# Head 0 in an order written out by hand, in a kernel for clustered attention and routed experts

## The chip, the cores and the metric

One core of one Trainium2 chip runs the whole kernel. The metric is the device time of one execution in microseconds (us), median of the runs of one kernel. The trace of one profiled execution stands beside it. Engines are named PE (TensorE), DVE (VectorE), ACT (ScalarE), POOL (GpSimd) and SP (SyncE, which issues most DMAs).

## What is computed

Attention in which a query sees only the keys of its own cluster, and behind it a mixture of eight experts with one expert for each token. Cut to what matters:

```python
# q, k, v: (2, 8, 768, 64); centroids: (8, 16, 64)
q_assign = argmax(normed(q) @ normed(centroids))   # likewise k_assign
mask = q_assign[..., :, None] == k_assign[..., None, :]
scores = where(mask, scale * q @ k.T, -1e9)
scores = scores - max(scores, -1)
attn = exp(scores); attn /= sum(attn, -1) + 1e-9
x = (attn @ v)                                     # to (1536 tokens, 512)
expert = argmax(x @ w_gate); gate = softmax(x @ w_gate)[expert]
out = gate * (relu(x @ w1[expert]) @ w2[expert])   # first 384 tokens of an expert, else 0
```

## The kernel before

The 16 (batch, head) items are called heads 0 to 15, and two of them, which lie in the two halves of the 128 partitions, a pair. A head has 768 queries and 768 keys: six tiles of 128 and two halves of 384.

For every head the kernel holds four arrays. `W` (high part of q, rows that hold the cluster mark) and `Y1` (high part of k, marks scaled by a large number) give masked scores by one matmul; `Qs` and `Y0` carry the low parts, and one row of `Qs` holds minus the maximum of each query, so that a second matmul into the same bank subtracts it. In the order listings these names carry buffer numbers: W_94, Y_98, Qs_102 and Y_106 belong to head 0, W_96, Y_100, Qs_104 and Y_108 to head 1, W_95, Y_99, Qs_103 and Y_107 to head 2, and W_97, Y_101, Qs_105 and Y_109 to head 3.

The work of one head:

- **Splitting** (`split`, steps 0 to 3): ACT copies the high parts (64x768), POOL subtracts the low parts in three pieces of 64x256 (`ql`, `Y0`), and SP issues DMAs that put pieces where the matmuls need them.
- **Clusters**, for a pair: scores against the centroids, arg-maxima on DVE (`cl_assign`: `cmx`, `ceq`, a product, `cm`, one-hot rows `ohb`), turned by six transposes on PE (`ctb`), scaled by one ACT instruction (`qkm`), and sent by four DMAs into the mark rows of `W` and `Y1` (`cl_back`).
- **Maxima** (`max_tile`): 12 times a matmul `m` (128x384) and a maximum over it on DVE (`mx`). Heads 1 to 15 join the 12 columns in `mxx`, turn them on PE (`mtp`), copy them with ACT (`mr`) and send the row to `Qs` by a DMA that SP issues (`max_chain`, `max_rows`). Head 0 does it in halves, without a DMA: `mxp` on DVE, transposes `mtd`, an ACT copy into `Qs`.
- **Scores** (`st_group`, 12 groups): two matmuls `s` into one bank, and ACT's exponential into `pf`.
- **Values** (`pv_batch`, two batches of six matmuls `o`) and **sums of rows** (`p_add` on DVE gives `acc`; `sum_strips`, eight matmuls `rsp`), then scaling and the way to the experts.

The main loop runs over heads i and groups g. In a group it issues the scores of head i, one maximum of a later head (two where (i, g) is in `TWICE`; the list `maxima` runs on over the heads), and what `hooks(i, g)` hangs there: the second batch of values of head i - 1, its additions and its sums at g = 2 (`G_B1`), the first batch of head i at g = 8 (`G_B0`; for head 0 at g = 11).

Order: the prologue is written in program order (`manual_schedule`). In head 0 a scheduler sets the order of all engines. From head 1 on `keep` holds PE, DVE and ACT to program order (`held`); POOL and SP stay with the scheduler. PSUM has three banks for `s` (`psS`), two for `m` (`psM`), one for `o` and `mtd` (`psO`) and two for the rest (`psT`), so a third `m` waits for the maximum of the first. `keep_warm` issues matmuls on ones (128x128) whose results nobody reads.

After head 15 come the experts, whose weights are loaded four blocks ahead; their loads are issued at fixed places of the program.

## Time and profile before

| | us |
|---|---|
| median of 3 runs | 473.61 (469.14 to 473.76) |
| profiled execution | 472.46 |
| its span, first to last instruction | 470.3 |

The profile's page counts PE busy for 444.9 us (95% of the span), DVE for 321.4, ACT for 272.7 and POOL for 138.5. A busy PE means that matmuls are under way, not that they run at the peak rate. In the timeline rows below the first number is the start in us from the start of the span, the second the time until the last of the row ends, and x the count of instructions; a matmul of full float32 is counted as two. The bracket at a row's end is the idle time of the engine ahead of it, and what ended that.

### The profile page before, as it was taken

To read this page: it belongs to the slowest core of one execution; us is meant where nothing else is said; L and a number is where in the kernel's file an instruction comes from. 1 tells how busy PE (TensorE), PEld (TensorE's weight loads), DVE (VectorE), ACT (ScalarE), POOL (GpSimd) and SP (SyncE) were. 2 spreads that over 40 slices of the span, in tenths; PEclk is the share of its full clock that TensorE was granted. 3 is DMA by queue.
4 is the path that set the end of the run, shared out by engine and by line. 5 is a ranking of instruction groups with operands and counts; after the bars stand their busy time and mean duration, and the time that the engine had idled before them with its cause. 6 is when DMAs were issued, how large, how long until landed. Compare 5 with 4: busy or idle time off the path is not lost. (4 is left out here: it accounts for less than half of the span.)

```text
span 470.3 us, 8149 instructions
## 1 busy us (share of the span) xinstructions
PE 444.9 (95%) x2832; PEld 346.0 (74%) x2832; DVE 321.4 (68%) x682; ACT 272.7 (58%) x548; POOL 138.5 (29%) x168
## 2 busy tenths in 40 slices
PE   8899999999999989999999978999999999999984
PEld 7764766576666656667755556899999999899963
DVE  6785868678686795787754565587867777687411
ACT  4752655565666555566564624577786868586430
POOL 6793345736334356433000130001010101011010
PEclk9998999999999999999999999999999999999998
DMA  8366449976341514423112058659697878865110
GB/s 281 87 172 214 148 94 344 340 220 231 85 118 35 161 50 147 130 45 88 42 50 91 17 203 307 206 175 289 234 276 252 252 259 238 260 212 204 37 36 18
DMA packets 31223, 78.14 MB, mean 166 GB/s; under 512 B 4678, under 2 KB 5024, under 8 KB 31172
## 3 DMA queue, kind: packets, MB, share of 16 engines
q1 hardware_dynamic: 26340, 61.33, 43.4%
q0 software_dynamic: 4832, 16.15, 8.9%
q8 instruction: 30, 0.49, 0.4%
q14 instruction: 21, 0.17, 0.1%
HBM read 50.46 MB, written 16.76 MB: 143 GB/s over the span
## 5 line engine op out<-in xcount | busy, mean ns | idle before, releaser
L342 DVE TENSOR_REDUCE mx<-m 128x1 f32<-128x384 f32 x192 | 102.5, 553 | 54.1 <-PE m L335 52.2
L400 ACT ACTIVATE pf<-s 128x384 f32<-128x384 f32 x192 | 90.6, 492 | 54.8 <-PE s L396 49.9
L137 DVE TENSOR_TENSOR ws<-wraw,ws 128x1024 fp32r<-128x1024 f32 x64 | 78.1, 1223 | 32.2 <-ACT ws L131 32.0
L395 PE MATMUL s<-W,Y 112*128 112x384 f32 (+1 forms) x192 | 73.7, 384 | 2.0 <-ACT pf L400 2.0
L335 PE MATMUL m<-Y,W 112*128 112x384 f32 (+1 forms) x192 | 68.6, 361 | 5.0 <-DVE mx L342 3.1
L909 PE MATMUL g<-xc,ws 128*128 128x416 f32 x224 | 70.0, 373 | 1.2 <-PEq L1046 0.3
L131 ACT ACTIVATE ws<-wraw 128x1024 fp32r<-128x1024 f32 x64 | 67.0, 1050 | 4.5 <-DMA wraw<-in_w_dram 4.5
L909 PE MATMUL g<-hc,ws 128*128 128x416 f32 x224 | 69.5, 371 | 0.0
L649 POOL DMA_INDIRECT out_dram<-y,row x17 | 18.0, 1057 | 171.5 <-ACT pt L917 110.9
L415 PE MATMUL o<-pf,v 128*64 128x384 f32 x360 | 66.2, 496 | 0.4 <-DVE r L457 0.4
L396 PE MATMUL s<-Qs,Y 97*128 97x384 f32 (+1 forms) x192 | 65.7, 342 | 0.4 <-issue 0.3
L910 PE MATMUL g<-xc,ws 128*128 128x208 f32 x224 | 58.1, 259 | 1.0 <-issue 1.0
L910 PE MATMUL g<-hc,ws 128*128 128x208 f32 x224 | 57.9, 259 | 0.0
L298 POOL TENSOR_TENSOR ql<-qv,W 64x256 fp32r<-64x256 f32 x45 | 39.9, 912 | 51.3 <-ACT W L311 26.2
L298 POOL TENSOR_TENSOR Y<-kv,Y 64x256 fp32r<-64x256 f32 x48 | 41.4, 889 | 43.3 <-ACT Y L316 42.0
L395 PEld LDWEIGHTS s<-W,Y 112*128 112x128 f32 (+1 forms) x192 | 36.5, 190 | 23.2 <-issue 16.6
L917 ACT ACTIVATE pt<-g 128x208 f32<-128x208 f32 x84 | 27.5, 340 | 32.0 <-PE g L910 27.9
L335 PEld LDWEIGHTS m<-Y,W 112*128 112x128 f32 (+1 forms) x192 | 36.5, 191 | 12.9 <-DVE mx L342 8.1
L909 PEld LDWEIGHTS g<-xc,ws 128*128 128x128 f32 x224 | 42.1, 188 | 3.3 <-issue 2.9
L415 PEld LDWEIGHTS o<-pf,v 128*64 128x64 f32 x360 | 23.4, 137 | 28.3 <-issue 24.8
L910 PEld LDWEIGHTS g<-xc,ws 128*128 128x128 f32 x224 | 42.8, 191 | 1.2 <-issue 1.2
L910 PEld LDWEIGHTS g<-hc,ws 128*128 128x128 f32 x224 | 42.7, 191 | 0.0
(206 smaller groups left out, 700.6 us busy)
## 6 DMA issues: line engine op xcount, KB each, us to landing
wraw<-in_w_dram SPq DMA_DIRECT2D x64, 512.0 KB
xd<-z POOLq DMA_DIRECT2D x7, 780.0 KB
row<-xd SPq DMA_DIRECT2D x18, 260.0 KB
qv<-in_qT_dram SPq DMA_DIRECT2D x8, 384.0 KB
kv<-in_kT_dram SPq DMA_DIRECT2D x8, 384.0 KB
v<-in_v_dram SPq DMA_DIRECT2D x8, 384.0 KB
Y<-Y SPq DMA_DIRECT2D x32, 96.0 KB
Qs<-W SPq DMA_DIRECT2D x16, 192.0 KB
```

The lines of the kernel that those rows point to most:

```text
L131: keep(nc.scalar.activation(out=w[:, 0], in_=raw[c], func=AF.Copy))
L137: keep(nc.vector.tensor_tensor(out=w[:, 1], in0=t, in1=w[:, 0].bitcast(F32), op=ALU.subtract))
L298: keep(eng.tensor_tensor(out=out[:, cc], in0=a[:, cc], in1=b[:, cc].bitcast(F32), op=ALU.subtract))
L335: keep(nc.tensor.matmul(out=m[:, 0:HALF], lhsT=W[0:KA[h % 2], t * P:(t + 1) * P], rhs=Y1[0:KA[h % 2], j * HALF:(j + 1) * HALF], start=True ...
L342: keep(nc.vector.tensor_reduce(out=mxt[h][:, j, t:t + 1], in_=m[:, 0:HALF], axis=AX.X, op=ALU.max))
L395: keep(nc.tensor.matmul(out=s[:, 0:HALF], lhsT=Y1[0:ka, ks], rhs=W[0:ka, qs], start=True, stop=False))
L396: keep(nc.tensor.matmul(out=s[:, 0:HALF], lhsT=Y0[0:kb, ks], rhs=Qs[0:kb, qs], start=False, stop=True))
L400: keep(nc.scalar.activation(out=pt[h, u][:, slot[0], slot[1]], in_=s[:, 0:HALF], func=AF.Exp, scale=1.0 / float(D) ** 0.5))
L415: keep(nc.tensor.matmul(out=ot[h][j * D:(j + 1) * D, 0:HALF], lhsT=vt[h // 2][:, h % 2, kt, :], rhs=pf[:, n, j], start=(kt == 0), stop=(kt ...
L909: nc.tensor.matmul(out=o, lhsT=w[0], rhs=x.rearrange("p o n -> p (o n)"), start=start, stop=False)
L910: nc.tensor.matmul(out=o[:, 0:RW], lhsT=w[1], rhs=x[:, 0], start=False, stop=stop)
L917: nc.scalar.activation(out=t, in_=o[:, RW:2 * RW], func=AF.Copy)
```

## The change

Head 0 leaves the main loop, and a function `opening` issues it in an order written by hand; `held` is set from its start, so PE, DVE and ACT follow program order there too.

- In the prologue the clusters of the second pair are assigned at once, on DVE, ahead of head 0's maxima (before: in four steps spread over head 0). The first copy of head 1's `W` moves ahead of the marks of head 0's keys, and these are written by one ACT instruction instead of one on DVE and one on ACT. The small constants `trib`, `ebr`, `dlr` and `run0` move from DVE to POOL, into the prologue.
- Head 0's 12 maxima and head 1's 12 come first on DVE. The two additions of head 0 and the maxima of head 2 stand behind them. Head 0's first batch of values starts behind the scores, the second stands in `opening` too instead of in head 1, with three maxima of head 2 between its pieces; two more stand between the sums in head 1. One maximum moves from the opening to group 8 of head 2.
- The split of head 2 begins in the prologue; that of head 3 follows behind head 0's scores, with its step 0 ahead of the row of head 1's maxima (`max_rows(1)`).
- 13 of the `keep_warm` matmuls go: 2 of 6 around head 0's key transposes, 1 of 4 among the first six maxima, 4 of 6 ahead of the first `mtd`, and the 6 among head 1's maxima.

```diff
     WARM1 = 1
-    WARM2 = 6
+    WARM2 = 2
     G_B0, G_B1, G_TURN, G_OUT = 8, 2, 5, 11
-    TWICE = {(0, g) for g in range(6)} | {(1, 2), (2, 2), (3, 2)}
+    TWICE = {(1, 2), (2, 2), (2, 8), (3, 2)}
...
-    def cl_back(pi):
-        tb = psT.tile([P, S], BF16, tag="t", name="ctb")
+    tb_t = {}
+
+    def cl_back_turn(pi):
+        tb = tb_t[pi] = psT.tile([P, S], BF16, tag="t", name="ctb")
         for t in range(NT):
             keep(nc.tensor.transpose(tb[:, t * P:(t + 1) * P], ohb[:, t, :], idb))
+
...
         if step == 0:
-            keep(nc.scalar.activation(out=W[a], in_=d["q"][a], func=AF.Copy))
+            if high:
+                keep(nc.scalar.activation(out=W[a], in_=d["q"][a], func=AF.Copy))
             ql[h] = work.tile([P, S], R32, tag="ql", name="ql", bufs=2)
             minus(eng, ql[h][a], d["q"][a], W[a])
...
-    def max_part(h, j, pool=psO, tag="o"):
-
-        mx = work.tile([P, TH], F32, tag="mxp", name="mxp")
+    def max_half(h, j):
+        mx = mxt[h, j] = work.tile([P, TH], F32, tag="mxp", name="mxp")
         ts = slice(j * TH, (j + 1) * TH)
         keep(nc.vector.tensor_tensor(out=mx, in0=mxt[h][:, 0, ts], in1=mxt[h][:, 1, ts], op=ALU.max))
+        if j == 1:
+            mxt.pop(h)
+
+    def half_row(h, j, warm=0):
+        mx = mxt.pop((h, j))
         br = MROW[h % 2]
-        tp = pool.tile([P, 512], F32, tag=tag, name="mtd")
-        if j == 0 and h == 0:
-            keep_warm(WARM2, tp)
+        tp = psO.tile([P, 512], F32, tag="o", name="mtd")
+        if warm:
+            keep_warm(warm, tp)
         for t in range(TH):
             keep(nc.tensor.transpose(tp[0:1, t * P:(t + 1) * P], mx[:, t:t + 1], ident))
         keep(nc.scalar.activation(
             out=pick(Qs_t, h)[br:br + 1, j * HALF:(j + 1) * HALF], in_=tp[0:1, 0:HALF], func=AF.Copy, scale=-1.0
         ))
-        if j == 1:
-            mxt.pop(h)
...
-    def pv_batch(h, u):
-        if u == 0:
+    def pv_batch(h, u, ns=range(TH)):
+        if (u, ns[0]) == (0, 0):
         pf = pt[h, u]
-        for n in range(TH):
+        for n in ns:
...
-    def sum_strips(h):
...
+            if between:
+                between()
...
         ebr, dlr = (const.tile([P, E], BF16, name=n) for n in ("ebr", "dlr"))
-        keep(nc.vector.memset(ebr, 0.0))
-        keep(nc.vector.memset(dlr, 0.0))
-        keep(nc.vector.tensor_copy(ebr[0:1], cs[0:1, C_EB:C_EB + E]))
+        nc.gpsimd.memset(ebr, 0.0)
+        nc.gpsimd.memset(dlr, 0.0)
+        nc.gpsimd.tensor_copy(ebr[0:1], cs[0:1, C_EB:C_EB + E])
...
-        if i == 0:
-            if g < 4:
-                next(gens["c"], None)
-            if g == 4:
-                cl_back(1)
-            if g in (2, 3, 4, 5):
-                split(2, g - 2)
-            if 6 <= g < 10:
-                split(3, g - 6)
...
         if g == G_B1 and i > 0:
-            pv_batch(i - 1, 1)
+            if i > 1:
+                pv_batch(i - 1, 1)
             if i > 1 and i != H + 2:
                 out_scale(i - 2)
-            p_add(i - 1, 1)
-            sum_strips(i - 1)
+            if i > 1:
+                p_add(i - 1, 1)
+            sum_strips(i - 1, ahead if i == 1 else None)
...
+        nc.gpsimd.tensor_copy(trib, cs[:, C_TRI:C_TRI + P])
+        first_rows()
...
-        cl_scores(1, 3, NT // 2, NT // 2 + 1)
+        cl_scores(1, 3, NT // 2, NT)
         split(0, 2)
+        cl_back0("k", tk)
         keep_warm(4, psM.tile([P, 512], F32, tag="m", name="warm"))
-        cl_back0("k", tk)
-        keep_warm(2, psM.tile([P, 512], F32, tag="m", name="warm"))
-        mask0("k", tk, 0, slice(0, HALF), nc.vector)
-        mask0("k", tk, 0, slice(HALF, S), nc.scalar)
+        nc.scalar.activation(out=pick(W_t, 1)[MAIN[1]], in_=pair[0]["q"][MAIN[1]], func=AF.Copy)
+        mask0("k", tk, 0, slice(0, S), nc.scalar)
+        for _ in cl_assign(1, nc.vector):
+            pass
         split(0, 3)
+        split(1, 0, high=False)
+        split(1, 1)
         mask0("q", tq, 1, slice(0, S), nc.scalar)
         mask0("k", tk, 1, slice(0, S), nc.scalar)
-        split(1, 0)
-        split(1, 1)
...
+        for k in range(NT):
+            first_max(k)
+        max_half(0, 0)
+        split(2, 0)
         for j in range(2):
             one_row(j, 1)
-        for k in range(NT):
-            if k in (1, 3):
-                t = NT // 2 + 1 + k // 2
-                cl_scores(1, 3, t, t + 1)
-            max_tile(0, k // 2, k % 2, *((psS, "s") if k % 5 < 3 else (psM, "m")), warm=0 if k in (1, 3) else WARM1)
-        max_part(0, 0)
-        gens["c"] = cl_assign(1, nc.vector)
-
-    def warm():
-        for k in range(NT, 2 * NT):
-            max_tile(0, k // 2, k % 2)
-        max_part(0, 1)
-        nc.vector.tensor_copy(trib, cs[:, C_TRI:C_TRI + P])
+        for k in range(NT, NT + 3):
+            first_max(k)
+        half_row(0, 0, WARM2)
+        cl_back_turn(1)
+
...
+        max_tile(0, k // 2, k % 2, *((psS, "s") if k % 5 < 3 else (psM, "m")), warm=WARM1 if k in (3, 4, 5) else 0)
+
+    def opening():
         load_pair(2)
-        first_rows()
+        split(2, 1)
+        for g in range(2 * NT):
+            if g == 4:
+                half_row(0, 1)
+            if g == 6:
+                cl_back_send(1)
+            st_group(0, g)
+            if g < 3:
+                max_tile(0, (g + NT + 3) // 2, (g + NT + 3) % 2)
+                if g == 2:
+                    max_half(0, 1)
+            else:
+                ahead()
+            if g == 3:
+                split(2, 2)
+                split(2, 3)
+        ahead(2)
+        pv_batch(0, 0, (0,))
+        ahead()
+        pv_batch(0, 0, (1, 2))
+        split(3, 0)
+        max_rows(1)
+        split(3, 1)
+        split(3, 2)
+        split(3, 3)
+        p_add(0, 0)
+        p_add(0, 1)
+        for n in range(TH):
+            pv_batch(0, 1, (n,))
+            ahead()
...
+    held[0] = True
+    def ahead(n=1, at=None):
+        for _ in range(n):
+            if maxima:
+                m, k = maxima.pop(0)
+                max_tile(m, k // 2, k % 2)
+                if k == 2 * NT - 1:
+                    max_chain(m)
+                    if at is not None:
+                        rows_at[at + 2] = m
+
...
-        for i in range(NH):
+        opening()
+        for i in range(1, NH):
             if i in (1, 3, 4, 5, 6, 7, 8):
                 tc.no_sync_barrier()
-            held[0] = i > 0
             for g in range(2 * NT):
                 st_group(i, g)
-                for _ in range(1 + ((i, g) in TWICE)):
-                    if maxima:
-                        n, k = maxima.pop(0)
-                        max_tile(n, k // 2, k % 2, warm=WARM1 if n == 1 and k % 2 == 0 else 0)
-                        if k == 2 * NT - 1:
-                            max_chain(n)
-                            rows_at[2 * NT * i + g + 2] = n
```

Three places, as the built programs have them.

DVE, from the marks of head 0's keys to the maxima (`L342` before and `L351` now is the maximum `mx`; `L241` to `L254` is the assignment). Before:

```order
L272 TENSOR_SCALAR Y_98<-ctk 16x384
L342 TENSOR_REDUCE mx<-m 128x1 x6
L355 TENSOR_TENSOR mxp<-mx 128x3
L1166 CAST trib<-cs 128x128
L623 MEMSET ebr 128x4
L624 MEMSET dlr 128x4
L628 MEMSET run_355 128x4
L625 CAST ebr<-cs 1x8
L241 TENSOR_REDUCE cmx<-ctp 128x24
L342 TENSOR_REDUCE mx<-m 128x1 x2
L244 TENSOR_TENSOR ceq<-ctp,cmx 128x384
L342 TENSOR_REDUCE mx<-m 128x1 x4
```

Now:

```order
L241 TENSOR_REDUCE cmx<-ctp 128x24
L244 TENSOR_TENSOR ceq<-ctp,cmx 128x384
L246 TENSOR_TENSOR ceq<-ceq,c16b 128x384
L249 TENSOR_REDUCE cm_270<-ceq 128x24
L254 TENSOR_TENSOR ohb<-ceq,cm_270 128x24x16
L351 TENSOR_REDUCE mx<-m 128x1 x6
L363 TENSOR_TENSOR mxp<-mx 128x3
L351 TENSOR_REDUCE mx<-m 128x1 x6
L363 TENSOR_TENSOR mxp<-mx 128x3
L351 TENSOR_REDUCE mx<-m 128x1 x12
L357 TENSOR_TENSOR mxx<-mx 128x6
L417 TENSOR_TENSOR acc<-pf 128x768 x2
```

The whole assignment stands ahead of the first maximum, and 24 maxima follow with only the two `mxp` between them.

SP, the DMAs around the row of head 1's maxima (`Qs_104<-mr`). Before:

```order
L308 DMA Y_107<-Y_99 32x768
L308 DMA W_97<-ql 32x768
L308 DMA Y_101<-Y_101 32x768
L287 DMA W_95<-qkm 16x768
L287 DMA Y_99<-qkm 16x768
L287 DMA W_97<-qkm 16x768
L287 DMA Y_101<-qkm 16x768
L376 DMA Qs_104<-mr 1x6x128
L308 DMA Qs_105<-W_97 64x768
```

Now:

```order
L316 DMA Y_107<-Y_99 32x768
L295 DMA W_95<-qkm 16x768
L295 DMA Y_99<-qkm 16x768
L295 DMA W_97<-qkm 16x768
L295 DMA Y_101<-qkm 16x768
L316 DMA W_97<-ql 32x768
L387 DMA Qs_104<-mr 1x6x128
L316 DMA Y_101<-Y_101 32x768
L316 DMA Qs_105<-W_97 64x768
```

The DMA of head 3's low part (`W_97<-ql`), which waits for POOL, now stands right ahead of the row.

PE, from the end of head 0 into head 1 (`L395` and `L396` before, `L406` and `L407` now are the scores `s`; `L415` and `L426` the values; `L335` and `L344` the maxima's `m`). Before:

```order
L335 MATMUL m<-Y_99,W_95 128x384 x6
L395 MATMUL s<-W_96,Y_100 128x384
L396 MATMUL s<-Qs_104,Y_108 128x384
L335 MATMUL m<-Y_99,W_95 128x384
L395 MATMUL s<-W_96,Y_100 128x384
L396 MATMUL s<-Qs_104,Y_108 128x384
L335 MATMUL m<-Y_99,W_95 128x384
L395 MATMUL s<-W_96,Y_100 128x384
L396 MATMUL s<-Qs_104,Y_108 128x384
L335 MATMUL m<-Y_99,W_95 128x384 x2
L415 MATMUL o<-pf,v 64x384 x6
L432 MATMUL rsp<-acc,onef 32x384 x2
```

Now:

```order
L384 MATMUL mtp<-cs,mxx 6x128
L426 MATMUL o<-pf,v 64x384 x2
L344 MATMUL m<-Y_99,W_95 128x384
L426 MATMUL o<-pf,v 64x384 x2
L344 MATMUL m<-Y_99,W_95 128x384
L426 MATMUL o<-pf,v 64x384 x2
L344 MATMUL m<-Y_99,W_95 128x384
L406 MATMUL s<-W_96,Y_100 128x384
L407 MATMUL s<-Qs_104,Y_108 128x384
L344 MATMUL m<-Y_99,W_95 128x384
L406 MATMUL s<-W_96,Y_100 128x384
L407 MATMUL s<-Qs_104,Y_108 128x384
```

The six `o` that stood behind head 1's third group now stand ahead of its first, between `mtp` and the scores that need the row; six `m` in a row there have become three among the `o`.

## Rows read from the trace of the kernel before

**Rows 1.** The page, TensorE's granted clock in 40 slices of the span (tenths of full speed).

```profile
PEclk9998999999999999999999999999999999999998
```

**Rows 2.** Windows of 3.4 us: busy time of each engine (x instructions), granted clock, DMA.

```profile
19.80:23.20 3.40, 2.77 (x11) 1.57 (x11) 2.80 (x6) 3.33 (x5) 3.23 (x6) 1.00 0.61 142
...
35.80:39.20 3.40, 2.46 (x7) 1.05 (x7) 2.90 (x6) 0.27 (x1) 0.00 (x0) 1.00 0.97 339
39.20:42.60 3.40, 3.37 (x11) 2.87 (x13) 1.87 (x5) 1.87 (x4) 0.00 (x0) 0.53 0.93 284
```

**Rows 3.** PE's timeline, head 0's first scores to head 1's fourth group; a wait in head 4.

```profile
19.67 0.41 PE L396 MATMUL s<-Qs,Y 97*128 97x384 f32 x1
...
35.51 0.27 PE L373 MATMUL mtp<-cs,mxx 128*6 128x128 f32 x1
...
39.23 0.53 PE L396 MATMUL s<-Qs,Y 128*128 128x384 f32 x1 [0.26 <-issue]
...
42.31 2.38 PE L415 MATMUL o<-pf,v 128*64 128x384 f32 x12
44.61 0.52 PE L432 MATMUL rsp<-acc,onef 128*32 128x384 f32 x2
...
46.68 0.44 PE L395 MATMUL s<-W,Y 128*128 128x384 f32 x1
...
47.14 0.34 PE L335 MATMUL m<-Y,W 112*128 112x384 f32 x1
...
47.67 0.34 PE L335 MATMUL m<-Y,W 112*128 112x384 f32 x1
...
94.15 0.41 PE L335 MATMUL m<-Y,W 112*128 112x384 f32 x1 [1.05 <-DMA W<-qkm]
```

**Rows 4.** DVE's timeline, prologue to head 1.

```profile
12.10 0.36 DVE L254 TENSOR_TENSOR ohb<-ceq,cm 128x192 bf16<-128x192 bf16 x1
...
14.85 3.14 DVE L342 TENSOR_REDUCE mx<-m 128x1 f32<-128x384 f32 x6 [1.11 <-PE m L335]
18.02 0.49 DVE L355 TENSOR_TENSOR mxp<-mx 128x3 f32<-128x3 f32 x1
...
19.18 0.54 DVE L241 TENSOR_REDUCE cmx<-ctp 128x24 f32<-128x384 f32 x1
...
23.73 0.84 DVE L246 TENSOR_TENSOR ceq<-ceq,c16b 128x384 bf16<-128x384 bf16 x1
...
27.43 1.03 DVE L254 TENSOR_TENSOR ohb<-ceq,cm 128x384 bf16<-128x384 bf16 x1
...
35.29 0.17 DVE L348 TENSOR_TENSOR mxx<-mx 128x6 f32<-128x6 f32 x1
...
42.97 0.95 DVE L406 TENSOR_TENSOR acc<-pf 128x768 f32<-128x768 f32 x1
```

**Rows 5.** ACT's timeline: head 0's first row of maxima, a copy, exponentials.

```profile
19.09 0.48 ACT L362 ACTIVATE Qs<-mtd 1x384 fp32r<-1x384 f32 x1 [1.41 <-PE mtd L361]
...
21.20 0.84 ACT L311 ACTIVATE W<-qv 64x768 fp32r<-64x768 f32 x1
...
23.45 1.26 ACT L400 ACTIVATE pf<-s 128x384 f32<-128x384 f32 x3
```

**Rows 6.** POOL's timeline: low parts, and a fill of zeros that it issues.

```profile
27.32 2.43 POOL L298 TENSOR_TENSOR ql<-qv,W 64x256 fp32r<-64x256 f32 x3
...
34.16 0.81 POOL L671 DMA_DIRECT2D xd<-z  x1
43.02 2.87 POOL L298 TENSOR_TENSOR ql<-qv,W 64x256 fp32r<-64x256 f32 x3 [8.05 <-ACT W L311]
```

**Rows 7.** SP's queue: a low part, the row of head 1's maxima, marks in head 4.

```profile
25.20 0.51 SPq L308 DMA_DIRECT2D W<-ql  x1
...
36.11 0.84 SPq L376 DMA_DIRECT2D Qs<-mr  x1
...
88.90 0.72 SPq L287 DMA_DIRECT2D Y<-qkm  x1
```

More of the change, by code (lines that the diff above doesn't have):

```diff
@@ L425, in pv_evict, with sum_strips @@
         keep(nc.scalar.activation(out=oT_t[h], in_=ot.pop(h)[:, 0:HALF], func=AF.Copy))
-    def sum_strips(h):
+    def sum_strips(h, between=None):
         ps = psT.tile([P, 512], F32, tag="t", name="rsp")
@@ L745, in hooks @@
                 cl_evict(strips_at(i))
-        if g == (G_B0 if i else 2 * NT - 1):
+        if g == G_B0:
             if i == NH - 1:
@@ L1172 @@
     tc.no_sync_barrier()
-    warm()
+    held[0] = True
[8 more added lines that the diff above has]
+                        rows_at[at + 2] = m
     with ExitStack():
@@ L1176 @@
         rows_at = {}
[L1177 removed]
+        opening()
+        for i in range(1, NH):
             if i in (1, 3, 4, 5, 6, 7, 8):
                 tc.no_sync_barrier()
[L1180 removed]
             for g in range(2 * NT):
                 st_group(i, g)
[L1183 to L1189 removed]
+                ahead(1 + ((i, g) in TWICE), 2 * NT * i + g)
                 if 2 * NT * i + g in rows_at:
```

11 lines of the change are left out of this document (8 added, 3 removed).

## The prediction

> **What bounds the kernel now.** The page's row of the granted clock comes first: it is 9 or 10 tenths nearly everywhere, and the one stretch that the change touches and that falls out of this is slice 4, which with 8 holds 35 to 47 us [rows 1]. Windows of 3.4 us narrow it down: from 35.8 to 39.2 PE ran only 7 matmuls, and in the next window the clock was 0.53, that is mostly the lower of its two levels, 1.2 instead of 2.4 GHz [rows 2]. So the kernel is bound by PE in most places, and in the opening by what PE waits for. The timelines tell what that is. Head 1 can't start before the row of its maxima is in place: its first scores complete their second matmul at 39.23 us [rows 3]. That row hangs on DVE, which joined the twelve maxima (`mxx`) at 35.29 [rows 4]; SP issued the row's DMA at 36.11 [rows 7]. DVE began head 0's maxima at 14.85, so the 24 maxima of two heads, which at 3.14 us for six are 12.6 us of work, took 20.4 us [rows 4]. In between stand the cluster assignment of the second pair, an addition, and waits for `m`. This chain, DVE to `mxx`, then PE, ACT, SP, the DMA and PE again, is what the change shortens or not. I follow it to the fourth group of head 1, at 46.68 [rows 3]; behind it both programs issue nearly the same PE work.
>
> **The change, part by part.**
>
> *The assignment ahead of the maxima.* The last one-hot rows of the first pair end at 12.46. The second pair's assignment is three instructions of 0.54, one of 0.84 and one of 1.03 us [rows 4], 3.5 together, so the maxima start at 15.95 instead of 14.85. That delay of 1.1 is paid once; before, the same work stood between the maxima. The single ACT instruction for the key marks and the four constants on POOL I count as nothing: they are done while DVE assigns, and DVE is what is late. If that cover went, the constants' 0.06 to 0.6 us would be back on DVE.
>
> *24 maxima in a row.* Six take 3.14, to 19.1, `mxp` 0.49, to 19.6. Before, the second matmul of the first scores came 1.65 behind the start of `mxp` (18.02 to 19.67, with the ACT copy from 19.09 for 0.48) [rows 3 to 5]; now that gives 20.75, and the tenth `m` stands behind it on PE, ready at 21.3, when DVE has been through the next three maxima (19.6 plus 1.6): 0.1 to 0.3 of waiting. The other six and the second `mxp` end near 23.5. PE then holds the next `m` behind the transposes of that `mxp` and two scores, about 1.0, and DVE has only one maximum of 0.52 in stock: 0.5 of waiting. ACT has the copy of head 2's `Y1` ahead of the first exponential, 0.84; that is made up, since three exponentials take 1.26 [rows 5] and three maxima 1.57. Twelve maxima of head 1 take 6.3, and near their end the last `m` stand behind the first values on PE; I allow 0.5. `mxx` is then done at 30.9 instead of 35.46.
>
> *The row.* `mtp` stands on PE behind four `o`; six take 2.16 or so (42.31 to 44.61 with the sums' start [rows 3]), four 1.5, and they start when the last `m` is issued, near 30.1: `mtp` at 31.6. Before, SP issued the row 0.6 behind `mtp`, and PE used it 3.12 behind that [rows 3, 7]. Now SP has `W_97<-ql` right ahead of it, a new wait: everything on SP's queue behind that DMA waits for POOL. POOL starts this low part when ACT has copied `W_97`, and ACT does that behind head 0's twelfth exponential. The groups run at the pace of the maxima, so the twelfth comes near 28.2, its exponential ends at 28.9 (three take 1.26), the copy of 0.84 at 29.7 [rows 5]; the low part takes 2.43 to 2.87 [rows 6], to 32.1 or 32.6, and the DMA ahead of the row 0.6 with its gap [rows 7]. The row is issued at 32.7 to 33.2, up to 1.0 later than `mtp` alone would allow. At 3.12 to its use that is 36.3 at the latest. From below it is bounded by PE itself, which behind `mtp` has six `o`, three `m` and the first matmul of the scores to do: 34.5. I take 35.5, about the middle: the row before was issued 1.1 behind the end of a fill of zeros [rows 6], which now stands behind it on POOL, but no row shows how much sooner it lands without that. Gain so far 3.7 us (2.9 to 4.7).
>
> The additions now run beside POOL's low part. One addition took 0.95 and the low part beside it 2.87 instead of 2.43 [rows 4, 6]; that is in the bounds above. The Trainium skill, "SBUF — State Buffer", section "Who interferes with whom", has DVE and GpSimd share a port pair as an exclusive lock, so that one instruction blocks the other whole. By that the low part would lose a full addition, 0.95 instead of 0.44, and the total would come out 0.5 smaller; the row speaks for the smaller loss.
>
> *Head 1 to its fourth group.* Before, 39.23 to 46.68, 7.45 us. Of it 3.08 went to 42.31, at the low clock, 2.30 to the six `o` (to 44.61), and 2.07 to sums and cluster matmuls [rows 3]. Now the three groups take 0.53 each (47.14 to 47.67 at full clock [rows 3]), 1.4 counted from the second matmul, with one more `m` and a wait for its bank 0.4; the `o` are gone, having filled PE's wait for the row; two `m` between the sums cost 0.36; the 2.07 stay. That makes 4.2 (4.0 to 4.7): gain 3.2, of which 2.3 are the `o` and 0.9 the clock. Late next is PE itself.
>
> *What comes back.* The maximum moved to group 8 of head 2 costs one matmul, 0.18, to 0.52 if DVE is late there: 0.2. The 13 removed warm-up matmuls give PE time in which it waits anyway: nothing. POOL's and SP's work for heads 3 to 5 keeps its place relative to the groups, and later transfers, the experts' weights too, are issued at places of the program; so the shift goes through to the end.
>
> Sum: 3.7 + 3.2 - 0.2 = 6.7 us (5.1 to 8.0).
>
> **The rivals.**
>
> *The clock falls in the opening.* From about 16.5 to 19.9 PE is paced by DVE: four `m`, three warm-up matmuls and the three transposes, 10 instructions. The window ahead of the low clock had 7, another with 11 kept 1.00 [rows 2]. That is nearer to the window that kept it. If it falls, three groups of nine matmuls cost more: 11 took 3.37 at the low level, 0.31 each, against three in 0.53, 0.18 each [rows 2, 3]. Nine times 0.13 less some waiting is 1.0: gain 5.7, 467.9 us. The Trainium skill, "TensorE: Matmul & The Clock Gate", section "What's actually happening", says that "the default state is throttled, and activity releases the throttle", which speaks against taking 13 warm-up matmuls away; the trace agrees in that 0.53 follows the thin window.
>
> *The row lands late.* A DMA of marks issued at 88.90 reached its matmul only at 94.15, 5.25 later [rows 3, 7]. With that the row issued at 33.0 is used at 38.25, 2.75 later than forecast: gain 3.95, 469.7 us. For it speaks that SP's queue is filled by then with the next head's transfers; against it that the fill of zeros comes later now.
>
> *Slower: the clock stays low from the first scores to head 1's fourth group.* In that stretch, 20.7 to 39.7, lie 30 `s`, 24 `m` and 12 `o` of two matmuls each: 78 times 0.13 is 10.1, and sums and clusters take their 2.07 again. Less the 3 us that PE waits there, that costs 9.2: 2.5 us slower than before, 476.1. It decides against the change once some 80% of the stretch runs at the low level (6.7 plus 3 of 12.2). Against it: once the maxima of head 1 begin, PE has a matmul every 0.18 us, the density at which the clock is 1.00 elsewhere.
>
> That the change doesn't do what it says I exclude: the listings show PE, DVE and ACT in the written order.
>
> **How the numbers follow.** The profiled execution took 472.46, 2.2 more than its span; minus 6.7 it is 465.8. It lies 1.15 below the median of the three runs, one of which, 469.14, lies 4.5 below. Against the median the forecast is 473.61 - 6.7 = 466.9. Chances: forecast 0.58, clock in the opening 0.22, late row 0.14, slower 0.04, nothing of the kind and no change 0.02. The likeliest case reaches from 465.6 to 468.5, the first rival to 469.0; with half of the late row's case and a scatter of 1.5 to 2 for the median of few runs the range is 463.9 to 470.9. One per cent, about what a measurement of this kernel can tell from no change, is 4.7 us, so faster means below 468.9: nearly all of the first case, four fifths of the second, a fifth of the third, 0.76. Slower 0.04, the rest, 0.20, the same.
>
> **What would show it.** In the profile after, the maxima start at 16 and `mxx` ends near 31; `W_97<-ql` is issued near 32.5 and the row right behind it; the second matmul of head 1's first scores comes near 35.5, its fourth group near 39.7; the clock is 1.00 in all windows from 16 to 43. I am wrong if `mxx` comes later than 33 (DVE waits more than I allow), if the row takes over 4 us to land, if a window shows 0.5, or if the fourth group comes 7 us earlier and the span doesn't shrink by that.

## The result, and the profile after

| | before | after |
|---|---|---|
| median, lowest to highest (us) | 473.13, 469.14 to 473.76 (4 runs) | 465.53, 465.24 to 467.38 (4 runs) |
| profiled execution, its span (us) | 472.46, 470.3 | 465.35, 463.6 |

The ratio is 0.988 (95% interval 0.984 to 0.992): faster by 0.8 to 1.6%, where 466.9 us and 0.76 for "faster" (below 468.9) were forecast. On later chips the kernel before had medians of 470.29, 471.05 and 470.45 over 25 to 29 runs; the gain there is nearer to 5 us than to 7.6. The medians count every execution, also the six that lie over 1.5% above the fastest of their kernel (1469.87 and 477.82 us of the kernel before, 491.28 of three_back and one each of b_assign, between2 and add_back), without which none moves by more than 0.4 us.

The page's row of the granted clock after has the weak slice 4 of [rows 1] gone; another stands in its place, slice 1:

```profile
PEclk9899999999999999999999998999999999999997
```

Windows narrow it down, as in [rows 2] (busy time of each engine, clock, DMA):

```profile
15.80:19.20 3.40, 2.36 (x10) 1.80 (x10) 3.37 (x8) 1.71 (x2) 3.40 (x6) 0.88 0.12 29
19.20:22.60 3.40, 3.28 (x18) 2.75 (x18) 2.31 (x5) 1.94 (x4) 3.23 (x5) 0.62 0.63 147
...
39.60:43.00 3.40, 3.40 (x28) 1.70 (x25) 1.29 (x3) 1.74 (x5) 3.30 (x5) 1.00 0.99 349
```

So in this profile the clock no longer falls at head 1 but in the opening, behind a stretch with 10 matmuls: the prediction's first rival has come. The timeline of DVE answers to [rows 4]:

```profile
12.19 0.36 DVE L254 TENSOR_TENSOR ohb<-ceq,cm 128x192 bf16<-128x192 bf16 x1
...
16.19 2.87 DVE L351 TENSOR_REDUCE mx<-m 128x1 f32<-128x384 f32 x6
19.09 0.53 DVE L363 TENSOR_TENSOR mxp<-mx 128x3 f32<-128x3 f32 x1
19.55 1.47 DVE L351 TENSOR_REDUCE mx<-m 128x1 f32<-128x384 f32 x3
22.11 1.65 DVE L351 TENSOR_REDUCE mx<-m 128x1 f32<-128x384 f32 x3 [1.09 <-PE m L344]
...
25.31 2.74 DVE L351 TENSOR_REDUCE mx<-m 128x1 f32<-128x384 f32 x5 [0.74 <-PE m L344]
28.30 2.75 DVE L351 TENSOR_REDUCE mx<-m 128x1 f32<-128x384 f32 x5 [0.25 <-PE m L344]
31.66 0.56 DVE L351 TENSOR_REDUCE mx<-m 128x1 f32<-128x384 f32 x1 [0.61 <-PE m L344]
32.25 0.55 DVE L357 TENSOR_TENSOR mxx<-mx 128x6 f32<-128x6 f32 x1
```

The 24 maxima take 16.0 us, from 16.19 to 32.22, where they took 20.4. DVE waits four times for `m`, 2.69 in all, where the prediction allowed 1.2. PE's timeline answers to [rows 3]:

```profile
21.34 0.52 PE L407 MATMUL s<-Qs,Y 97*128 97x384 f32 x1
...
32.99 0.27 PE L384 MATMUL mtp<-cs,mxx 128*6 128x128 f32 x1
33.20 0.87 PE L426 MATMUL o<-pf,v 128*64 128x384 f32 x4
33.99 0.45 PE L344 MATMUL m<-Y,W 112*128 112x384 f32 x1
...
36.79 0.34 PE L407 MATMUL s<-Qs,Y 128*128 128x384 f32 x1
...
38.06 0.91 PE L344 MATMUL m<-Y,W 112*128 112x384 f32 x2
38.90 0.52 PE L443 MATMUL rsp<-acc,onef 128*32 128x384 f32 x2
...
41.99 0.45 PE L406 MATMUL s<-W,Y 128*128 128x384 f32 x1
...
62.60 0.44 PE L344 MATMUL m<-Y,W 112*128 112x384 f32 x1 [0.41 <-DVE mx L351]
...
90.93 0.41 PE L344 MATMUL m<-Y,W 112*128 112x384 f32 x1 [1.69 <-issue]
...
236.62 0.49 PE L463 MATMUL rtp<-cs,rs 128*128 128x128 f32 x3
```

Between `mtp` and the second matmul at 36.79 no row shows a wait: PE has values and `m` to do until the scores of head 1, and the row of maxima is not what it waits for. Nor was it the main wait before. There PE stood idle between `mtp` and its second matmul at 39.23 for 0.26 us right ahead of that matmul, and for 0.48 and 0.18 us for DVE's maxima:

```profile
36.79 0.91 PE L335 MATMUL m<-Y,W 112*128 112x384 f32 x2 [0.48 <-DVE mx L342]
37.88 0.91 PE L335 MATMUL m<-Y,W 112*128 112x384 f32 x2 [0.18 <-DVE mx L342]
```

SP, POOL and ACT stand in the order that the prediction had ([rows 5 to 7]): the copy of `W_97` behind the twelfth exponential, the low part, its DMA, and the row right behind it:

```profile
29.69 0.84 ACT L320 ACTIVATE W<-qv 64x768 fp32r<-64x768 f32 x1
```

```profile
30.67 2.11 POOL L306 TENSOR_TENSOR ql<-qv,W 64x256 fp32r<-64x256 f32 x3 [5.25 <-issue]
```

```profile
32.80 0.51 SPq L316 DMA_DIRECT2D W<-ql  x1
33.59 0.84 SPq L387 DMA_DIRECT2D Qs<-mr  x1
```

**Where the 6.7 us between the two spans lie.** At head 1's fourth group the kernel after is ahead by 4.7 (46.68 against 41.99). It loses 0.85 at head 2's eighth group, where the moved maximum waits (62.60), and 0.6 in head 4, at the `m` that needs the marks (a wait of 1.69 instead of 1.05 [rows 3]; in the other profiles this wait is 1.34 to 1.48 in the order before and 0.65 to 1.79 in the order after, so the 0.6 is not clear of scatter); some of that comes back, and late in the attention, at the `rtp` of 236.62, which stands at 240.47 before, it is ahead by 3.85. The last 2.85 come behind it, mostly in the experts, where both kernels do the same: 229.8 us from there to the end before, 227.0 after. The repeats show that most of this part is chance.

### The profile page after: what moved, and what is told of

Same layout as the page of the kernel before. It is cut to its first block, busy times and chain, and to the rows that moved or that the text cites. A ratio compares the mean times of both kernels' runs of the same rounds, so it can differ in the third digit from the quotient of the medians.

```text
span 463.6 us, 8096 instructions
## 1 busy us (share of the span) xinstructions
PE 439.9 (95%) x2806; PEld 342.8 (74%) x2806; DVE 321.4 (69%) x676; ACT 274.0 (59%) x548; POOL 139.5 (30%) x173
## 5 line engine op out<-in xcount | busy, mean ns | idle before, releaser
L351 DVE TENSOR_REDUCE mx<-m 128x1 f32<-128x384 f32 x192 | 103.0, 553 | 50.5 <-PE m L344 48.9
L406 PE MATMUL s<-W,Y 112*128 112x384 f32 (+1 forms) x192 | 73.6, 383 | 1.0 <-ACT pf L411 1.0
L344 PE MATMUL m<-Y,W 112*128 112x384 f32 (+1 forms) x192 | 67.8, 357 | 4.9 <-DVE mx L351 2.7
L426 PE MATMUL o<-pf,v 128*64 128x384 f32 x360 | 65.3, 495 | 0.4 <-DVE r L470 0.4
L407 PE MATMUL s<-Qs,Y 97*128 97x384 f32 (+1 forms) x192 | 65.2, 339 | 0.0
L406 PEld LDWEIGHTS s<-W,Y 112*128 112x128 f32 (+1 forms) x192 | 36.5, 190 | 21.8 <-issue 16.6
L344 PEld LDWEIGHTS m<-Y,W 112*128 112x128 f32 (+1 forms) x192 | 36.2, 189 | 14.9 <-DVE mx L351 8.7
L426 PEld LDWEIGHTS o<-pf,v 128*64 128x64 f32 x360 | 23.0, 136 | 27.6 <-issue 23.9
```

The source lines that it names most:

```text
L344: keep(nc.tensor.matmul(out=m[:, 0:HALF], lhsT=W[0:KA[h % 2], t * P:(t + 1) * P], rhs=Y1[0:KA[h % 2], j * HALF:(j + 1) * HALF], start=True ...
L351: keep(nc.vector.tensor_reduce(out=mxt[h][:, j, t:t + 1], in_=m[:, 0:HALF], axis=AX.X, op=ALU.max))
L406: keep(nc.tensor.matmul(out=s[:, 0:HALF], lhsT=Y1[0:ka, ks], rhs=W[0:ka, qs], start=True, stop=False))
L407: keep(nc.tensor.matmul(out=s[:, 0:HALF], lhsT=Y0[0:kb, ks], rhs=Qs[0:kb, qs], start=False, stop=True))
L426: keep(nc.tensor.matmul(out=ot[h][j * D:(j + 1) * D, 0:HALF], lhsT=vt[h // 2][:, h % 2, kt, :], rhs=pf[:, n, j], start=(kt == 0), stop=(kt ...
```

## The experiments

Kernels differ in when the prologue ends, so I count from t0, the end of the one-hot rows of the first pair's keys (DVE `ohb`), to `mtp` of head 1, and on to head 1's fourth group. "Low clock" names the windows of 3.4 us with under 0.9. The prediction's times, counted so, are 19.1, 8.1 and 27.2.

| kernel | t0 | t0 to `mtp` | `mtp` to 4th group | sum | low clock | median (runs), lowest |
|---|---|---|---|---|---|---|
| before | 12.46 | 23.05 | 11.17 | 34.22 | 39 to 43 | 473.13 (4), 469.14 |
| again_before | 15.40 | 24.49 | 9.61 | 34.10 | 23 to 33 | 470.90 (8), 468.95 |
| b_hold | 12.31 | 23.78 | 11.21 | 34.99 | 40 to 46 | 470.14 (12), 469.10 |
| b_assign | 12.45 | 24.80 | 8.98 | 33.78 | 16 to 23 | 472.17 (10), 469.55 |
| after | 12.55 | 20.44 | 9.00 | 29.44 | 16 to 23 | 465.53 (4), 465.24 |
| again_after | 12.54 | 21.13 | 8.99 | 30.12 | 19 to 23 | 465.54 (2), 464.73 |
| warm | 12.90 | 20.50 | 8.99 | 29.49 | none | 465.76 (10), 464.38 |
| values_back | 15.41 | 20.49 | 9.92 | 30.41 | none | 468.08 (10), 465.49 |
| assign_back | 12.69 | 21.54 | 8.98 | 30.52 | 23 to 29 | 466.93 (8), 465.77 |
| add_back | 12.56 | 20.29 | 8.99 | 29.28 | none | 465.19 (10), 464.17 |
| three_back | 12.88 | 23.62 | 9.89 | 33.51 | 23 to 33 | 468.70 (10), 466.56 |
| hold | 13.21 | 19.78 | 8.99 | 28.77 | none | 465.25 (6), 464.13 |
| between2 | 13.10 | 19.78 | 8.99 | 28.77 | none | 466.03 (12), 464.51 |
| hold_best | 12.97 | 19.77 | 8.98 | 28.75 | none | 464.63 (5), 463.80 |

**The two kernels again, unchanged.**

> The kernel before, unchanged, profiled again. In the two profiles the change gained 4.7 us up to head 1's fourth group, 3.85 of it reached the end of attention, and the experts took 226.98 us (from the last transposes of a full head's sums to the end) against 229.83, 2.85 less, though the change doesn't touch them. Theory one (spread): the experts' time differs from execution to execution, so this repeat shows another value between 226.5 and 231, and the opening the same as before: the second matmul of head 1's first scores at 39.2 plus or minus 0.5, the fourth group at 46.7, or earlier by about 1 if the clock doesn't fall there. Theory two (systematic): the experts of the kernel before always take near 229.8, within 0.5.

> The changed kernel, unchanged, profiled again. Theory one (spread): opening as in the first profile, or up to 1.0 us shorter if the clock doesn't fall at 18.5 us; the experts' time again between 226.5 and 231 and not tied to the kernel. Theory two (systematic): the experts take 227.0 within 0.5, below the kernel before in every profile.

The way to the fourth group repeats within 0.7 in either kernel, so by these four profiles 4.0 to 4.8 of it is the change's (by b_hold and hold, further down, 6.2: the clock fell in the first and not in the second). From that `rtp` to the end the kernel before took 227.4 us this time; so did b_hold and b_assign (227.4 and 227.3), and the ten profiles with the order after took 225.8 to 227.0. 229.8 stands alone. So 2.4 of the 6.7 between the first two spans was chance; whether the some 0.4 that is left in the experts belongs to the change stays open. A second thing came up: t0 was 15.40 instead of 12.46, whose cause is below.

**warm.** Twelve warm-up matmuls are put back:

```
-    WARM2 = 2
+    WARM2 = 6
...
+        if k == 5:
+            keep_warm(5, psT.tile([P, 512], F32, tag="t", name="warm"))
-        max_tile(0, k // 2, k % 2, ..., warm=WARM1 if k in (3, 4, 5) else 0)
+        max_tile(0, k // 2, k % 2, ..., warm=WARM1 if k >= 3 else 0)
```

> The changed kernel with 12 more matmuls on ones in the prologue, in time that PE waits: five ahead of the sixth maximum, one before each of the maxima seven to nine, four more ahead of the first transposes of a half. Theory (the clock fell in the opening for want of PE work and cost about 1.0): granted clock 1.00 from 15 to 24 us, the second matmul of the first scores at 20.7 instead of 21.34, head 1's fourth group at 41.0 to 41.5 instead of 41.99, 464.5 to 465.2 us. Rival (PE has slack there and DVE alone sets the pace, so the low clock cost nothing): clock 1.00, fourth group unchanged within 0.2, 465.5. Second rival: the matmuls on ones delay the maxima's matmuls, fourth group up to 0.5 later.

The clock stays at 1.00 and the time is the same, as the first rival had it. By itself that looks as if the fall cost nothing. But hold, between2 and hold_best come through the opening without a fall and without these matmuls: `mtp` stands 19.77 to 19.78 behind t0 there, against 20.44 and 21.13 with a fall and 20.50 here. So the fall came with 0.7 and 1.35 us in the two profiles that had it: up to the second `mxp` it cost 0.7 and 1.06, and the other 0.3 of the longer one is that `mxp` itself (0.65 us instead of 0.34 in hold). The kernel warm is 0.7 behind hold for two reasons: the warm-up matmuls stand on PE ahead of the first scores (8.60 behind t0 to their second matmul, 8.24 in hold), and here too the second `mxp` is long, 0.69 us. No run shows what makes it long. Nor is it shown that the warm-up matmuls kept the clock up, since add_back and values_back had no fall without them either.

**values_back.** Head 0's second half of the values, and its addition, go back behind head 1's second group; the three maxima stay.

```
-            if i > 1:
-                pv_batch(i - 1, 1)
+            pv_batch(i - 1, 1)
...
-        p_add(0, 1)
-        for n in range(TH):
-            pv_batch(0, 1, (n,))
-            ahead()
+        ahead(3)
```

> The changed kernel with the second batch of head 0's values and its second addition put back into head 1's third group, where they were before; the three maxima between them stay. My prediction's step: the batch fills a wait of PE for the row of maxima, so moving it back loses 2.3 us less what PE waits then: the row, issued near 33.6 or a little earlier, is used 2 to 3.1 later, at 35.6 to 36.7, and the fourth group comes at 43.3 to 44.3 instead of 41.99, 467 to 468 us. Rival (PE was the bound, the row was in place long before, and the batch only changes places): second matmul of head 1's first scores at 34.5, fourth group at 42.0, 465.5 us.

Now PE does wait for the row, as its timeline shows:

```profile
35.90 0.27 PE L384 MATMUL mtp<-cs,mxx 128*6 128x128 f32 x1
...
37.10 0.45 PE L344 MATMUL m<-Y,W 112*128 112x384 f32 x1 [0.58 <-DVE mx L351]
37.39 0.34 PE L406 MATMUL s<-W,Y 128*128 128x384 f32 x1
38.50 0.41 PE L407 MATMUL s<-Qs,Y 128*128 128x384 f32 x1 [0.77 <-DMA Qs<-mr]
```

SP issued the row at 36.50; it was used 2.0 later, not 3.12 as before [rows 3, 7]. In again_before and b_assign PE had no wait for the row at all, and used it 2.69 and 2.12 behind its issue:

```profile
40.49 0.84 SPq L376 DMA_DIRECT2D Qs<-mr  x1
43.18 0.33 PE L396 MATMUL s<-Qs,Y 128*128 128x384 f32 x1
```

```profile
37.85 0.84 SPq L376 DMA_DIRECT2D Qs<-mr  x1
39.97 0.34 PE L396 MATMUL s<-Qs,Y 128*128 128x384 f32 x1
```

From `mtp` to the fourth group this kernel takes 9.92, with the values ahead 9.00: moving them is worth 0.9, where the prediction had the six `o`, 2.3, as gone. They fill two waits, 0.58 and 0.77, and some 0.4 of that is lost again, since an `m` between values takes PE 0.38, against 0.18 between scores. Up to `mtp` PE and DVE do what they do in the kernel after. That this took 20.49 without a fall of the clock, 0.7 more than in hold, goes with a wait of DVE for the second pair's cluster scores, right behind t0; the maxima start 0.7 later for it:

```profile
16.61 0.56 DVE L241 TENSOR_REDUCE cmx<-ctp 128x24 f32<-128x384 f32 x1 [1.20 <-PE ctp L178]
```

Its median is 2.5 above the kernel after's, its lowest time 0.76 above again_after's; the profile has t0 at 15.41, so the median carries the prologue's scatter.

**assign_back and b_assign.** The place of the second pair's assignment, undone in the kernel after, and done alone in the kernel before.

```
assign_back, against after
-        for _ in cl_assign(1, nc.vector):
-            pass
+        gens["c"] = cl_assign(1, nc.vector)
...
+            if g < 4:
+                next(gens["c"], None)
```

```
b_assign, against before
-        cl_scores(1, 3, NT // 2, NT // 2 + 1)
+        cl_scores(1, 3, NT // 2, NT)
...
+        for _ in cl_assign(1, nc.vector):
+            pass
```

> The kernel after with the second pair's cluster assignment spread over head 0's groups again, its marks sent in one piece behind group 6, the maxima thus starting at once. Times are counted from the end of the one-hot rows of the first pair's keys (12.5 us in the kernel after) to the fourth group of head 1; that took 29.4 and 30.1 in two profiles of the kernel after, 34.1 and 34.2 in two of the kernel before. Theory 'DVE's work is the same, only its order differs': the 3.5 us of the assignment leave the front and return between the maxima of head 1, so the joined maximum of head 1 ends within 0.7 us of where it does now, and the stretch takes 29.0 to 30.8; the median stays within 1.5 us of the kernel after, some 4 to 6 us below the kernel before. Rival 'the place of the assignment is the gain': the assignment between the maxima makes DVE wait for more than its own work, as in the kernel before, and the stretch takes 32 us or more, the median 2.5 us or more above the kernel after.

> The kernel before with one part of the change alone: the second pair's assignment whole and ahead of head 0's maxima, its scores in one go; everything else stays as before. From the end of the one-hot rows of the first pair's keys to the fourth group of head 1 the kernel before took 34.1 and 34.2 us. Theory 'the place of the assignment alone is worth nothing': 33.6 to 34.8 us, median within 1.5 us of the kernel before. Rival 'it is the larger part': 32 us or less, median 2 us or more below the kernel before.

Alone the place is worth nothing (33.78 against 34.1 and 34.2, and a median that is no lower), though the three profiles have their falls of the clock in different places. Within the written order it is worth 0.4 to 1.1 against the two profiles with a fall, and 1.75 against those without; the median says 1.4. Part of that is the clock, which in assign_back is low in two windows, behind a stretch in which PE waits 1.08 and 1.28 us while DVE assigns:

```profile
22.60:26.00 3.40, 2.12 (x9) 1.87 (x9) 2.36 (x6) 0.97 (x2) 2.99 (x4) 0.64 0.87 286
26.00:29.40 3.40, 3.40 (x22) 2.95 (x21) 2.44 (x5) 2.63 (x6) 0.00 (x0) 0.86 0.46 119
```

All five profiles with the assignment between the maxima have a stretch of low clock somewhere in the opening, and only three of the nine with the assignment ahead. Both ways to the fourth group lie where the theories had them (30.52 and 33.78); the joined maximum of assign_back comes 0.4 and 1.1 later than in the two profiles of the kernel after, where 0.7 was allowed. So the order on DVE alone gives nothing, and gives some 1 us once the maxima run in a row.

**add_back.** The first addition goes back between head 1's sixth and seventh maximum.

```
+            if g == 8:
+                p_add(0, 0)
...
-        p_add(0, 0)
```

> The kernel after with one part undone: the addition of head 0's first two groups of weights (DVE, 1.24 us beside the maxima in the kernel before) is made again between head 1's sixth and seventh maximum, not behind the joined maximum. Measured from the end of the one-hot rows of the first pair's keys: five profiles of the kernel after or of near kin have head 1's fourth group at 28.8 to 30.1 us, the kernel before at 34.1 and 34.2; the first maxima row of head 1 (its transposes) stands at 20.4 and 21.1 in the kernel after, 23.1 and 24.5 in the kernel before. Theory 'DVE is the pace up to the joined maximum': the transposes come 0.9 to 1.5 us later, the fourth group 0.8 to 1.4 us later (30.3 to 31.0), the median 0.7 to 1.5 us above the kernel after (465.5). Rival 'DVE waits for PE there anyway (2.7 us in the kernel after), so the addition fills a wait': under 0.4 us at both places, median within 0.6 us.

On DVE's timeline the addition takes the place of a wait of 0.25 and delays what follows by the rest; the last wait for `m` is 0.61 as in the kernel after:

```profile
27.30 0.95 DVE L417 TENSOR_TENSOR acc<-pf 128x768 f32<-128x768 f32 x1
28.17 2.74 DVE L351 TENSOR_REDUCE mx<-m 128x1 f32<-128x384 f32 x5
31.52 0.56 DVE L351 TENSOR_REDUCE mx<-m 128x1 f32<-128x384 f32 x1 [0.61 <-PE m L344]
```

There was no fall of the clock, so it compares with 19.78 and 28.77: 0.5 at both places, between the two theories, and not to be seen in the median.

**three_back.** The edits of values_back, assign_back and add_back together.

> The kernel after with three parts undone at once: the second pair's assignment spread between the maxima again, head 0's second half of the values products behind head 1's second group again, the addition between head 1's maxima again. What then is left of the change in the opening is the hand-written order (the maxima and groups of heads 0 and 1 on PE and DVE) and the 13 warm-up matmuls taken out. One by one the first two cost 0.4 to 1.1 and 0.3 to 1.0 us on the way to head 1's fourth group. Theory 'the parts add up, and the written order is the largest': the fourth group comes 31.2 to 32.6 us behind the one-hot rows (28.8 to 30.1 in the kernel after, 34.2 before), 1.6 to 3 us ahead of the kernel before; median 467.5 to 469.5. Rival 'the three parts are the change': 33.6 to 34.4 us, median within 1.5 us of the kernel before.

The profile lies next to the rival's range (33.51 against 33.6 to 34.4, with the clock low from 23 to 33 us), the times say the theory: the median lies 3.2 above the kernel after's and 1.75 below the 470.45 of the kernel before beside it. By the lowest times, values_back lies 0.8, assign_back 1.0 and this kernel 1.8 above again_after's 464.73, so those two parts would add up; the kernel before's lowest, 468.2, would leave some 1.7 for the written order of maxima and groups. But a lowest time falls with the number of runs, and these are the lowest of 2 to 25. By the profiles the three parts undone together cost 4.1, more than their sum, part of it the clock. So what the written order gives is a remainder, argued and not shown: 1.7 by these times, 0.6 to 1.5 by the profiles.

**hold and b_hold.** In two of the first six profiles DVE's two instructions on the constants took long, whatever the kernel. Of the kernel after and again_before:

```profile
5.24 0.83 DVE L1080 TENSOR_SCALAR csq<-cs,css 128x128 f32<-128x128 f32 x1
5.44 0.70 DVE L1126 CAST idb<-cs 128x128 bf16<-128x128 f32 x1
```

```profile
5.23 2.87 DVE L1074 TENSOR_SCALAR csq<-cs,css 128x128 f32<-128x128 f32 x1
5.43 2.74 DVE L1118 CAST idb<-cs 128x128 bf16<-128x128 f32 x1
```

Both hang together with POOL's four zero fills, which run from 5.26 to 8.2 in the kernel after and to 8.0 in again_before. In the kernel after the second fill took 0.87 instead of 0.73, as if DVE had been let in there; in the two profiles with the long pair every fill took 0.73, and the pair ended at 8.1 to 8.2, behind the last. The edit holds the second set of fills behind DVE's cast:

```
-        for lst in (W_t, Y1_t, Qs_t, Y0_t):
-            zero_rows(lst, 1)
...
+        hold = work.tile([P, 1], BF16, tag="hold", name="hold", bufs=1)
+        nc.gpsimd.tensor_copy(hold, idb[:, 0:1])
+        for lst in (W_t, Y1_t, Qs_t, Y0_t):
+            zero_rows(lst, 1)
```

> The kernel after with GpSimd's second set of zero fills, the copy of the triangle and the constants held behind DVE's cast of the identity (a copy of one of its columns on GpSimd stands ahead of them). In the profiles so far DVE's two instructions on the constants took 0.84 and 0.70 us, or, when GpSimd's fills ran from their start to 8.2 us, 2.87 and 2.74, and everything behind came 2.3 to 2.9 us later; which of the two came had nothing to do with the kernel (before: one profile each; after: twice the short one). Theory 'GpSimd's fills block DVE': with the fills held the two instructions take 0.84 and 0.70 in every execution, the one-hot rows of the first pair's keys end at 12.4 to 13.1, and the median falls 0.5 to 2 us below the kernel after's, with a smaller scatter. Rival 'the long ones have another cause': the long pair can still come with the fills held, and the median stays within 0.5 us. If the fills held come too late for the first transfers that need zeroed rows, the first scores come later than 9 us behind the one-hot rows (8.8 in the kernel after).

> The kernel before with the same hold on GpSimd's second set of fills and nothing else. In one of two profiles of the kernel before the two DVE instructions beside the fills took 2.87 and 2.74 us and the one-hot rows ended at 15.4 instead of 12.5 us; its times spread from 468.2 to 475. Theory 'the fills make this spread': the instructions take 0.29 and 0.22, the one-hot rows end at 12.4 to 13.3 in the profile, the times fall into a band of about 3 us and the median 0.7 to 2 us below the kernel before's. Rival 'the spread comes from elsewhere, or the fills held make the first transfers late': median within 0.5 us of the kernel before, the band as wide as before.

Of hold, DVE:

```profile
5.26 0.29 DVE L1080 TENSOR_SCALAR csq<-cs,css 128x128 f32<-128x128 f32 x1
5.46 0.22 DVE L1122 CAST idb<-cs 128x128 bf16<-128x128 f32 x1
```

The instructions alone take 0.28 to 0.29 and 0.22, in the one profile of each of the three kernels with the hold, less than the 0.84 and 0.70 that hold's theory had: the fills block DVE, and even the short pair was blocked for half a microsecond. The Trainium skill, "SBUF — State Buffer", section "Who interferes with whom", says that a cast or tensor_scalar of DVE can enter two-port modes, in which it and GpSimd shut each other out for a whole instruction. These rows agree in that DVE comes in only behind a whole fill; they show more, since the long pair came in behind four in a row. The scatter is smaller with the hold: b_hold's 12 runs lie within 2.2 us, the 29 of the kernel before beside them within 4.6; hold's and hold_best's 11 lie below 466.8, while between2, without the hold, has 4 of 12 from 470.1 to 471.6. The long pair moves t0 by 2.9, which is less than that, so the rest of those 5 to 6 us is not explained. The medians, though, hardly move (470.14 against 470.45; 465.25 against 465.5), as the rivals had it: behind the short pair DVE waits 0.82 us for ACT's `cnf` in any case. As the two kernels with the least scatter, b_hold and hold put the change at 4.9 us, though they ran on two chips; on the chip of hold the kernel before lies 5.8 above it.

**between2.** Head 2's extra maximum goes between the sums of its third group.

```
-    TWICE = {(1, 2), (2, 2), (2, 8), (3, 2)}
+    TWICE = {(1, 2), (2, 2), (3, 2)}
...
-            sum_strips(i - 1, ahead if i == 1 else None)
+            sum_strips(i - 1, ahead if i == 1 else None, ahead if i == 2 else None)
```

> The kernel after with the one extra maximum of head 2's eighth group (which made PE wait 0.41 us and cost 0.85 us in the distance to the kernel before) put between the two sums of head 2's third group instead. Theory 'the extra maximum stalls PE since its bank isn't free': the wait goes, and from head 1's fourth group to head 3 the kernel is 0.4 to 0.8 us shorter; median 0.4 to 0.8 below the kernel after's. Rival 'one more maximum costs the same wherever it stands, since DVE sets the pace of the groups': the 0.4 us appears at the new place, and the median stays within 0.3 us.

The wait at 62.60 is gone: the `m` ahead of head 2's first values runs right behind the scores.

```profile
62.24 0.36 PE L344 MATMUL m<-Y,W 112*128 112x384 f32 x1
62.54 2.16 PE L426 MATMUL o<-pf,v 128*64 128x384 f32 x12
```

Counted from the fourth group, head 2's values start 0.3 earlier: the wait goes, as the theory has it, but the gain is under its 0.4 to 0.8. Head 4's `rtp` comes 0.55 earlier than in the kernel after (49.79 against 50.35 behind it), but only 0.1 earlier than in hold (49.90), since the wait for the marks differs from profile to profile. The median, with its 4 long runs, can't show it.

**hold_best.** hold, between2, and head 1's last three maxima ahead of all of head 0's first values.

> The kernel after with the three edits that gained something in a profile: GpSimd's second set of fills held behind DVE's cast of the identity (0.29 and 0.22 us for the two instructions instead of 0.84 and 0.70, or 2.87 and 2.74), head 2's extra maximum between the sums of its third group, and the last three maxima of head 1 ahead of all of head 0's first values on PE, which takes one or two values groups (0.18 to 0.4 us each) from the way to the joined maximum. Theory 'all three hold': the joined maximum ends 0.3 to 0.8 us earlier behind the one-hot rows than in the kernel after (19.9 to 20.3 us there), median 463.9 to 465.2, all executions within 3 us of each other. Rival 'the maxima moved ahead wait for their banks, since DVE is the pace': no gain at the joined maximum; median 464.9 to 465.6. In either case it beats both kernels or equals the kernel after.

464.63 us, ratio 0.988 (0.985 to 0.990) to the kernel before, all five runs between 463.8 and 464.9. It beats the kernel before clearly and the kernel after by 0.9, which the intervals don't separate. The maxima moved ahead did no good by themselves. DVE's last wait is gone and the joined maximum ends 18.9 behind t0 (19.6 in hold), as the theory has it, but `mtp` stands at 19.77, as in hold:

```profile
31.36 0.51 DVE L357 TENSOR_TENSOR mxx<-mx 128x6 f32<-128x6 f32 x1
```

```profile
30.65 2.16 PE L426 MATMUL o<-pf,v 128*64 128x384 f32 x12
32.74 0.27 PE L384 MATMUL mtp<-cs,mxx 128*6 128x128 f32 x1
```

The four `m` ahead of these values wait 1.1 us for DVE's maxima. Then PE runs its values back to back up to `mtp`: from the last `m` on PE is the bound, not the maxima.

## Why the prediction was right, and where it was off

Up to `mtp` the chain it named was the right one; behind `mtp` PE's own work set the time, not the row. The sign and the range held, and the median lies 1.4 below the forecast. But that is partly luck, twice over: the 473.61 that the forecast starts from lies some 3 us above the later medians of the kernel before, and the gain of 6.7 was too large by nearly 2, so the two errors cancel in part; and 2.4 of the 6.7 between the two spans came in the experts, by chance. On the way to head 1's fourth group 6.9 were forecast, and the profiled pair shows 4.8. The 2.2 that are missing (29.44 against 27.24), step by step:

- **The maxima in a row.** They started at 16.19, where 15.95 was forecast. DVE's waits were 2.69, not 1.2; 0.7 of that is the clock (the first wait is 1.09, in hold 0.39). Without the fall of the clock `mtp` stands 19.78 behind t0 (hold), 0.64 later than forecast: the last `m` 0.33, and the four values behind it, with that `m`, 1.81 instead of 1.5. The last of DVE's waits, 0.61, costs nothing, as hold_best shows.
- **The clock.** This was the first rival, at a price of 1.0, held less likely than the clock's staying up. It came in the two profiles of the kernel after, and `mtp` stood 0.66 and 1.35 later there than in hold. The argument from the nearest window failed: 10 and 12 matmuls stood in the window from 15.8 to 19.2 of the two profiles that fell, 11 to 17 in four that didn't (hold, between2, hold_best, add_back), so their number doesn't tell the two apart.
- **The row.** The order on SP's queue was as forecast, 32.80 and 33.59, but the new wait for POOL's low part cost nothing: the row was issued 0.60 behind `mtp`, as before. The low part took 2.11, not 2.43 to 2.87; it was done at 32.78, and the additions began at 32.72, so they didn't run beside it. From `mtp` to the scores 3.8 passed where 3.9 were forecast, and 3.72 before: this step gained nothing, and not for the reason given, since PE's own work filled it. The 3.12 from the row's issue to its use, taken from before, was no landing time that holds elsewhere: 2.0 was enough in values_back, and at most 2.12 in b_assign. The second rival, a late row, is out.
- **Head 1 to its fourth group.** 5.2 instead of 4.2, the largest single miss. The pair of `m` behind the third group took 0.84 (allowed 0.4 and its part of 1.4), the two between the sums 0.75 (allowed 0.36), and sums and cluster matmuls 2.34 (allowed 2.07).
- **The six `o`.** Counted as a gain of 2.3; values_back says 0.9. They filled waits of 0.58 and 0.77, and took the rest of their time from PE ahead of the scores. In the order before, six `m` filled much of that wait already. The other part of the step was the clock: `mtp` to the fourth group took 11.17 before, with the low clock there, and 9.61 and 8.98 in again_before and b_assign, without it, against 9.00 after. So without the fall this step gained 0 to 0.6.
- **What comes back.** The moved maximum cost 0.85 in the spans' distance, not 0.2. That the shift "goes through to the end" did not hold in head 4, where a wait for the marks was 0.64 longer in this pair, which is within the scatter of the other profiles.
- **The removed warm-up matmuls** at nothing: right in the sum, by effects that cancel. The kernel warm has no fall of the clock and loses as much by its matmuls on PE and a longer `mxp`.

So the size is nearer to 4.9 us (hold against b_hold) than to 6.7, just under the lower bound of the sum, 5.1; against the kernel before on the same chip it is 4.75 (again_after, 2 runs) to 5.8 (hold). The 7.6 of the first medians rests on four runs before, three of which lie high, 472.7 to 473.8. The term that was most off is the six `o`, 2.3 for 0.9. What the change's parts are worth singly, by the table: values 0.9, the addition 0.5, the assignment 0.4 to 1.75 with the clock; what is left for the written order stays open within 1 us.

## What to carry to other kernels

Work that is moved into a wait is worth at most the wait, not its own length: look for the stretch in which the waiting engine shows no row at all, and count only that. Compare stages from a marker behind the prologue's scatter, and repeat the kernel before until its own spread is known, before a gain of one per cent is split into parts.

## What was not expected of the hardware

Two DVE instructions of 0.29 and 0.22 us took 0.83 and 0.70, or 2.87 and 2.74, beside four zero fills of GpSimd. Which of the two came differed between two profiles of the kernel before and moved t0 by 2.9 us. With the fills held the profiles of all three kernels tried show 0.28 to 0.29 and 0.22. And the granted clock fell in one stretch of 3 to 10 us in the opening of eight of fourteen profiles, at places that differ between executions of the same kernel (39 and 23 us in the kernel before, the second with t0 2.9 later), so a clock's price read in one profile belongs to that profile.
